# Three more attention groups scored by four strips of 32 rows, with their keys kept in finished output tiles

## The chip, the cores and the metric

The kernel runs on one core of one Trainium2 chip. The metric is the device time of one execution in microseconds. The kernel before takes 632.41 us as the median of 3 runs (631.19 to 633.22).

## The reference

Two independent blocks share the launch; their outputs stand side by side. The first is attention with 16 query heads of width 28 over one shared key and value head. The second is a two-dimensional spectral filter.

```python
B, S, D, H = 1, 2048, 448, 16          # Dh = 28
q = (x @ wq).reshape(B, S, H, Dh).transpose(0, 2, 1, 3)
k = x @ wk;  v = x @ wv                # one head, shared by the 16
scores = einsum("bhqd,bkd->bhqk", q, k) * Dh ** -0.5
o = einsum("bhqk,bkd->bhqd", softmax(scores, -1), v)
a = o.transpose(0, 2, 1, 3).reshape(B, S, H * Dh) @ wo
X = rfft2(x2, axes=(-2, -1)) * (w_r + 1j * w_i)
b = irfft2(X, s=(S, D), axes=(-2, -1))
return concatenate([a, b], -1)
```

## The kernel before, in words

**The stages.** The first 72 us project queries, keys and values and start the forward transform of the spectral block. The rest is one long attention stage, into which the remaining spectral work and the output projections are woven, and a short tail.

**Groups and steps.** The queries are cut into 4 chunks of 512 rows (`c`) and 4 sets of 4 heads (`g`). One pair (c, g) is a group; there are 16, numbered here from the 1st to the 16th in the order of work (the program's own number, `4 * c + g`, starts at 0). A group has 16 steps, one for each block of 128 keys (`kc`), so there are 256 steps. A step makes four score tiles of 128 keys by 512 queries, one for each head, each in one bank of PSUM; exponentiates them on ScalarE into SBUF tiles `p`; and multiplies them with the values `vs` on TensorE into bank 7 (line 1190). Seven banks are left for scores and for other work.

**Two ways to score.** Queries and keys are split into a high and a low part (`qh`, `ql`, `kh`, `kl`), and the score is kh·qh + kh·ql + kl·qh.

- *Strips* (function `strips`, lines 1131 to 1166). Each head has 28 rows in a strip of 32 partitions, and the keys stand four times, once in each strip. The step issues 12 matmuls of 32 rows: three passes over four strips (line 1141). Four strips work side by side in the array. The exponentials of a step are taken of one bank, of two neighbouring banks at once, and of one bank (lines 1155 and 1157), where two of the free banks are neighbours; else of four single banks. The order is strict: one step's strips, then the values of the step two before it.
- *Stacked* (function `score`, line 1119). The three products (and kl·ql) stand below each other in the 128 rows: the keys in one tile `ka` = [kh, kh, kl, kl], the queries of a group in a tile `qa` that holds [qh, ql, qh, ql] of each head. One matmul of 128 rows gives one head's tile, so a step is 4 matmuls, with four exponentials of one bank each (line 1175). `build_q` prepares `qa` of the next group: three VectorE operations (lines 194 to 196) and nine DMAs on SyncE's queue (lines 213 and 214).

Before the change the first 5 groups are strips (`STRIPS = 5`) and the other 11 are stacked. `HOME` names groups whose queries are split straight into a `qa` tile's space.

**What sets the order.** All engines run an order that the program writes out while it is built. A small clock model (`clk`, `free`, `end`) decides in the main loop (from line 1259) when to score, when to multiply with the values and when to put in other TensorE work, which is called a fill here. In stacked groups the values come in blocks of two steps, called a pair here (8 scores, then 2 steps of values), or, where there is work to fill in, in blocks of four steps with up to three or four fills between the scores. The fills are the output projections of finished chunks (`w_unit`, line 1039, 44 matmuls for each of the first three chunks) and the last part of the inverse transform (`z_unit`, `y_unit`, lines 941 and 967). No fill is put into strips. When all scores are issued, the first 36 matmuls of the last chunk's projection follow (`partial`: 12 pieces of 3 matmuls), then the last head set's.

**Where the keys stand.** `kh` and `kl` for strips live in the first buffers of the pools tagged `oh` and `ol`. Each pool has two buffers; the normed outputs of a chunk (`oh[c]`, `ol[c]`) rotate through the same buffers. A chunk's outputs are read for the last time by its output projection.

Of the kernel before, what the change touches and what calls it, by code (L numbers as in the profile page):

```python
# [12 lines left out]
F32 = mybir.dt.float32  # L13
# [19 lines left out]
LEAD = 7  # L33
WARM = 8, 8
FIRST = 8
STRIPS = 5
HOME = {1: 0, 3: 1, 4: 0}
PLACES = (3, 5, 6, 8, 9, 10)


# [57 lines left out]
def kernel(ctx: ExitStack, tc: tile.TileContext, t: dict):  # L98
    nc = tc.nc
# [98 lines left out]
    def build_q(c, g):  # L198
        n = 4 * c + g
        qt = qp.tile([128, CW], F32, name="qt")  # L200
        if n in HOME:
            qh, ql = (slots[HOME[n]][:, p] for p in range(2))
        else:
            qh = qp.tile([128, CW], F32R, name="qh")
            ql = qp.tile([128, CW], F32R, name="ql")
        split_q(qt, qh, ql, c, g)
        if n < STRIPS:
            qa[c, g] = qh, ql
            return
        q = qa[c, g] = slots[n % 2]  # L210
        for i in range(4):
            for p, src in enumerate((qh, ql)):
                nc.sync.dma_start(q[32 * p:32 * p + 32, i].bitcast(F32), src[32 * i:32 * i + 32].bitcast(F32))
        nc.sync.dma_start(q[64:128].bitcast(F32), q[0:64].bitcast(F32))
# [543 lines left out]
    def stacked_keys():  # L758
        for p, k in enumerate((kh, kh, kl, kl)):
            r = slice(32 * p, 32 * p + 32)  # L760
            nc.sync.dma_start(ka[r].bitcast(F32), k[r].bitcast(F32))

    t1v = t1.rearrange("(r k) l u (n f) -> r (k l u) n f", r=2, f=113)

    def spread(i):
# [294 lines left out]
    def w_unit(c, k):  # L1060
        def go(g):
            def f(b):
                wo_mm(bank[b][:, :D], c, k, (g,))
                if g == NG - 1:
                    after(clk["pe"] + 0.9, 0.65, out, b)
            return f

        def out(b):
            wo_out(bank[b][:, :D], c, k)
            free[b] = clk["dve"] + 0.1  # L1070
        return [(0.605 if g else 0.403, go(g)) for g in range(NG)]


# [56 lines left out]

    def strips(st):
        c, g, kc = steps[st]
        bs = heapq.nsmallest(4, range(7), key=free.__getitem__)
        mid = next(((a, a + 1) for a in sorted(bs[:3]) if a + 1 in bs[:3]), None)
        if mid and st:
            bs = [b for b in bs[:3] if b not in mid] + [*mid, bs[3]]
        qh, ql = qa[c, g]
        for n, (k, q) in enumerate(((kh, qh), (kh, ql), (kl, qh))):
            for i in range(4):
                r = slice(32 * i, 32 * i + 32)  # L1140
                mm(bank[bs[i]], k[r, kc * 128:(kc + 1) * 128], q[r], start=(n == 0), stop=(n == 2))  # L1141
        switch("r")
        t0 = clk["pe"] + (0.11 if clk["new"] else 0.0)
        at = []
        for b in bs:
            t0 = max(t0 + 0.005, free[b])
            free[b] = inf
            at.append(t0 + 0.46 + 0.49)
        clk["pe"], clk["new"] = t0 + 0.69, False
        ends, sides = [pp.tile([128, 2, CW], F32, name="p") for _ in range(2)], (0, 3)  # L1150
        for i in range(4):
            pt[4 * st + i] = ends[0][:, i // 3] if i in sides else ends[1][:, i - 1]
        for i, n in ((0, 1), (1, 2), (3, 1)) if mid and st else ((i, 1) for i in range(4)):
            if n == 2:
                nc.scalar.activation(ends[1], banks[:, bs[1]:bs[1] + 2], AF.Exp, scale=SCALE)  # L1155
            else:
                nc.scalar.activation(pt[4 * st + i], bank[bs[i]], AF.Exp, scale=SCALE)  # L1157
            a = max(clk["act"], at[i + n - 1], vend[st - 4] if st > 3 else 0.0)
            clk["act"] = a + (0.904 if n == 2 else 0.49)
            for m in range(i, i + n):  # L1160
                end[4 * st + m] = clk["act"] + 0.163
                free[bs[m]] = clk["act"] + 0.153
        if kc == 0:
            after(clk["pe"] + 3.0, 1.7, build_q, *order[4 * c + g + 1])

    half = []
# [1 line left out]
    def exps():  # L1168

        while waiting and waiting[0][0] < 4 * done_steps + P_BUFS:  # L1170
            i, b, at = waiting.popleft()
            if i % 2 == 0:
                half[:] = [pp.tile([128, 2, CW], F32, name="p")]
            p = pt[i] = half[0][:, i % 2]
            nc.scalar.activation(p, bank[b], AF.Exp, scale=SCALE)  # L1175
            a = max(clk["act"], at, vend[(i - P_BUFS) // 4] if i >= P_BUFS else 0.0)
            clk["act"] = a + 0.490
            end[i] = a + 0.593 + 0.06
            free[b] = a + 0.593 + 0.05

    def values(o, n):
        while taken_out[0] < o // 16:
            vector(clk["dve"] + 0.5)
        switch("v")
        if held[0]:
            piece()
        for st in range(o, o + n):
            c, g, kc = steps[st]
            for i in range(4):
                mm(bank[7][32 * i:32 * i + 32], vs[:, kc], pt.pop(4 * st + i), start=(kc == 0), stop=(kc == 15))  # L1190
            clk["pe"] = max(clk["pe"], end[4 * st + 3]) + 0.86
            vend[st] = clk["pe"] + 0.15
            if kc == 15 and st < 255:
                after(clk["pe"] + 0.4, 0.72, group_out, c, g)
        clk["new"] = False
# [5 lines left out]
    def first_fill():  # L1201
        pb = fft1_mm(FIRST - 1)
        clk["pe"] += 1.0
        free[6] = inf
        fft1_out(FIRST - 1, pb)
        clk["dve"] = max(clk["dve"], clk["pe"] + 0.5) + 1.5
        free[6] = clk["dve"] + 0.1
# [11 lines left out]
        after(1.0 + 3.0 * (q - FIRST), 0.0, late_load, q)  # L1219
        after(6.0 + 9.0 * (q - FIRST), 1.35, late_fold, q, 0)  # L1220

    sc, since, gap = 64 * STRIPS, 0, 2
    parts, tail = deque((k, g) for k in range(4) for g in range(NG - 1)), {}

    def partial():
# [7 lines left out]
        wo_mm(tail[k], NC - 1, k, (g,))  # L1233
        spent(0.605)

    def size():
        left = 16 - done_steps % 16
        rich = sum(map(len, work["w"])) * 0.6 + len(work["z"]) * 0.88 + (len(cur[0][0]) * 0.6 if cur[0] else 0.0) > 1.0
        b = 4 if rich else 2
        return left if left < b + 2 else b  # L1240
# [1 line left out]
    total = 12 * 2.22 + 16 * (0.88 + 0.73)  # L1242

    def share(n):
        return max(1.8, n * (total - done[0]) / max(250 - done_steps, 3)) if n > 2 else 0.0

    done_steps, quota = 0, 0.0
    for k in range(16 * STRIPS):
        if k:
            vector(clk["pe"])  # L1250
        strips(k)
        if k == 0:
            first_fill()
        if k > 1:
            values(done_steps, 1)
            done_steps += 1
            exps()
    n = size()
    while done_steps < 256:
        vector(clk["pe"])  # L1260
        hold()
        need = 4 * (done_steps + n)
        t_v = end[need - 1]
        soon = min(free) <= clk["pe"] + 0.05
        more = sc < 1024
        if t_v <= clk["pe"] + 0.05 and (sc >= min(need + LEAD, 1024) or not soon):
            values(done_steps, n)
            done_steps += n
            exps()
            n = size()  # L1270
            since, gap, quota = 0, 2, share(n)
        elif can_fill() and quota > 0 and since >= EARLY and gap >= 2 and (cur[0] or soon):
            t0 = done[0]
            fill()
            quota -= done[0] - t0
            gap = 0
        elif more and soon:
# [163 lines left out]
```

## Time and profile before

| | us |
|---|---|
| median of 3 runs | 632.41 |
| profiled execution | 635.41 |
| its span | 633.6 |
| TensorE busy | 626.5 |
| ScalarE busy | 543.1 |
| VectorE busy | 343.1 |
| strips, first five groups (start of the second step to the first stacked score) | 75.7 to 227.0 |
| stacked, eleven groups (first stacked score to the last value matmul) | 227.0 to 619.0 |
| tail | 619.0 to 633.6 |

The profiled execution is 3.0 us longer than the median of the runs, and 1.8 us longer than its span. In the timeline a row gives start, duration, engine, line, operation and how many stand in it; the idle time before it stands in brackets with what ended it. One value matmul in the program appears as two in the trace, so "x16" on line 1190 is two steps. Matmuls overlap, so the distance from one start to the next tells the pace, not the sum of the durations.

### The profile page before, as it was taken

How to read it: one execution, taken by the hardware profiler on the slowest of the kernel's cores; microseconds unless marked ns; L12 is line 12 of the kernel's file. 1: busy time of each engine (PE TensorE's matmuls, PEld its weight loads, DVE VectorE, ACT ScalarE, POOL GpSimd, SP SyncE). 2: the span in 40 equal slices, each digit the busy share in tenths (PEclk: the TensorE clock that was granted, in tenths of full speed). 3: DMA queues.
4: the chain of work that ended last, by engine and by line, in shares of the span. 5: the costliest groups of instructions: out<-in, count | busy, mean ns of one | idle time of the engine just before them, and what ended most of it. 6: DMA issues, size and time to landing. Idle time of an engine off the chain costs nothing.

```text
span 633.6 us, 12824 instructions
## 1 busy us (share of the span) xinstructions
PE 626.5 (99%) x4976; PEld 333.5 (53%) x4976; DVE 343.1 (54%) x684; ACT 543.1 (86%) x1023; POOL 90.5 (14%) x167
## 2 busy tenths in 40 slices
PE   8999999999999999999999999999999999999997
PEld 6877633333333346554445656657564446564445
DVE  6898522979788988897732533226462202330104
ACT  4645599999999998789998878888779998889991
POOL 1021130202121201010323012021110101010200
PEclk9999799999999999999999999999999999999999
DMA  8746695001033422130673242152523020140002
GB/s 305 267 127 181 156 251 202 17 19 46 2 94 91 108 52 62 63 82 24 186 247 98 93 116 97 47 145 69 157 82 69 31 68 31 39 108 2 16 1 87
DMA packets 29367, 62.34 MB, mean 98 GB/s; under 512 B 6689, under 2 KB 16257, under 8 KB 28469
## 3 DMA queue, kind: packets, MB, share of 16 engines
q1 hardware_dynamic: 21338, 39.97, 22.1%
q0 software_dynamic: 7536, 20.98, 10.9%
q8 instruction: 39, 0.64, 0.4%
q10 hardware_dynamic: 432, 0.57, 0.2%
q14 instruction: 22, 0.18, 0.1%
HBM read 30.58 MB, written 16.30 MB: 74 GB/s over the span
## 4 chain that ended last, share of the span: by engine, by line
PE 88%; ACT 0%; issue 0%; DVE 0%; ACTq 0%
PE banks L1190 38%; PE banks L1119 28%; PE banks L1141 12%; PE banks L1039 5%; PE banks L941 2%; PE banks L967 2%; PE banks L1318 0%; PE banks L167 0%; ACT p L1155 0%; ACT yb L1054 0%; DVE yb L1057 0%; ACTq L1055 0%; ACT p L1157 0%
## 5 line engine op out<-in xcount | busy, mean ns | idle before, releaser
L1175 ACT ACTIVATE p<-banks 128x512 f32<-128x512 f32 x704 | 350.6, 713 | 38.6 <-PE banks L1190 22.5
L1190 PE MATMUL banks<-p,vs 128*32 128x512 f32 x2048 | 249.6, 599 | 0.0
L1119 PE MATMUL banks<-qa,ka 128*128 128x512 f32 x704 | 196.5, 407 | 0.0
L1119 PEld LDWEIGHTS banks<-qa,ka 128*128 128x128 f32 x704 | 124.7, 188 | 79.9 <-ACT p L1175 56.4
L1190 PEld LDWEIGHTS banks<-p,vs 128*32 128x32 f32 x2048 | 51.8, 109 | 116.4 <-issue 113.6
L1157 ACT ACTIVATE p<-banks 128x512 f32<-128x512 f32 x168 | 93.4, 624 | 2.7 <-PE banks L1141 2.6
L1155 ACT ACTIVATE p<-banks 128x1024 f32<-128x1024 f32 x76 | 79.4, 1045 | 0.0
L996 DVE COPY qraw<-banks 128x512 f32<-128x512 f32 x15 | 10.4, 692 | 72.4 <-PE banks L1190 72.4
L1001 POOL DMA_DIRECT2D sd<-qraw x15 | 9.0, 597 | 256.7 <-DVE qraw L996 256.7
L1043 DVE COPY ya<-banks 128x448 f32<-128x448 f32 x12 | 7.5, 625 | 67.3 <-PE banks L1039 34.0
L1141 PEld LDWEIGHTS banks<-qa,kh 32*128 32x128 f32 x384 | 14.5, 183 | 40.2 <-ACT p L1157 40.2
L1141 PE MATMUL banks<-qa,kh 32*128 32x512 f32 x384 | 35.5, 441 | 0.0
L824 DVE SCALAR_TENSOR_TENSOR X<-w,X 128x226 f32<-128x226 f32 (+2 forms) x72 | 34.1, 473 | 2.4
L1009 POOL DMA_DIRECT2D R<-rd x60 | 30.5, 515 | 30.5 <-DMA rd<-rs 30.5
L973 DVE COPY w<-banks 128x256 f32<-128x256 f32 x16 | 6.8, 424 | 37.4 <-PE banks L967 36.7
L327 ACT ACTIVATE qraw<-banks 128x512 f32<-128x512 f32 x16 | 9.4, 599 | 19.2 <-PE banks L323 19.1
L323 PE MATMUL banks<-xh,wqh 128*128 128x512 f32 x64 | 24.6, 417 | 0.6 <-DVE xh L271 0.6
L323 PE MATMUL banks<-xh,wql 128*128 128x512 f32 x64 | 23.2, 394 | 0.0
L949 DVE CAST zh<-banks 113x512 fp32r<-113x512 f32 (+1 forms) x16 | 11.0, 688 | 21.3 <-ACT p L1175 17.6
L1039 PE MATMUL banks<-woh,oh 128*128 128x448 f32 x60 | 22.2, 370 | 0.0
L1039 PE MATMUL banks<-wol,oh 128*128 128x448 f32 x60 | 21.9, 365 | 0.0
L1141 PEld LDWEIGHTS banks<-qh,kh 32*128 32x128 f32 x128 | 7.0, 190 | 27.9 <-ACT p L1157 25.1
(130 smaller groups left out, 701.2 us busy)
## 6 DMA issues: line engine op xcount, KB each, us to landing
qa<-qa SPq DMA_DIRECT2D x11, 512.0 KB
xb<-xb SPq DMA_DIRECT2D x8, 512.0 KB
ob<-yo SPq DMA_DIRECT2D x16, 256.0 KB
t<-bs SPq DMA_DIRECT2D x16, 226.0 KB
X<-t POOLq DMA_DIRECT2D x8, 452.0 KB, 12.7
wf<-w POOLq DMA_DIRECT2D x8, 452.0 KB, 3.7
c<-t POOLq DMA_DIRECT2D x8, 452.0 KB, 4.0
R<-rd POOLq DMA_DIRECT2D x60, 56.0 KB, 2.2
```

Source lines behind the costliest of these rows:

```text
L323: mm(pq[c, g], w[:, j, gs], x[:, j], start=(j == 0 and n == 0), stop=(j == 3 and n == 1))
L824: todo(226 * n, lambda d=d, q=q: STT(both(d), t[0].rearrange("p r n f -> p r (n f)"), q, both(a), op0=ALU.mult, op1=ALU.add))
L941: mm(pz[:w, j], fb["c2", q % 2][:, e, j, :w], fb["fi", q % 2][:, j], start=True, stop=True)
L967: mm(py[:, k], c[:w, kind], z, start=(n == 0), stop=(n == 2))
L1009: nc.gpsimd.dma_start(R[32 * i:32 * i + DH], rd[i:i + 1].to_broadcast([DH, CW]))
L1039: mm(p, x[c][:, g, s], w[:, m], start=(g == 0 and n == 0), stop=(g == NG - 1 and n == 2))
L1119: mm(bank[b], ka[:, kc * 128:(kc + 1) * 128], qa[c, g][:, h], start=True, stop=True)
L1141: mm(bank[bs[i]], k[r, kc * 128:(kc + 1) * 128], q[r], start=(n == 0), stop=(n == 2))
L1155: nc.scalar.activation(ends[1], banks[:, bs[1]:bs[1] + 2], AF.Exp, scale=SCALE)
L1157: nc.scalar.activation(pt[4 * st + i], bank[bs[i]], AF.Exp, scale=SCALE)
L1175: nc.scalar.activation(p, bank[b], AF.Exp, scale=SCALE)
L1190: mm(bank[7][32 * i:32 * i + 32], vs[:, kc], pt.pop(4 * st + i), start=(kc == 0), stop=(kc == 15))
```

## The change

The set of strip groups becomes a list: the first five groups and the 8th, 13th and 16th (program numbers 7, 12, 15). `kh` and `kl` no longer exist when these run, so their keys are copied: as soon as a chunk's output projection has read its `oh` and `ol` tiles for the last time, four DMAs on SyncE's queue (`copy_keys`) fill these two tiles with kh and kl, four strips each, from the stacked `ka`. The first chunk's tiles serve the 8th group, the second's the 13th, the third's the 16th. The queries of the three groups go straight into a `qa` tile's space on VectorE, without the nine DMAs each.

The main loop now enters strips when all earlier scores are issued and the values are at most two steps behind; it issues them without fills, and it sizes blocks of stacked steps so that they end at the entrance. The weight that spreads the fills over the steps (`share`) now counts up to step 234, not 250.

```diff
-STRIPS = 5
-HOME = {1: 0, 3: 1, 4: 0}
+STRIPS = 0, 1, 2, 3, 4, 7, 12, 15
+HOME = {1: 0, 3: 1, 4: 0, 7: 1, 12: 0, 15: 1}
+KEYS = {7: 0, 12: 1, 15: 2}
...
-        if n < STRIPS:
+        if n in STRIPS:
             qa[c, g] = qh, ql
             return
...
+    spread_keys = {-1: (kh, kl)}
+
+    def copy_keys(c):
+        spread_keys[c] = [x[c].rearrange("p g n -> p (g n)") for x in (oh, ol)]
+        for k, d in enumerate(spread_keys[c]):
+            for u in range(2):
+                nc.sync.dma_start(d[64 * u:64 * u + 64].bitcast(F32), ka[64 * k:64 * k + 64].bitcast(F32))
...
             wo_out(bank[b][:, :D], c, k)
             free[b] = clk["dve"] + 0.1
+            if k == 3:
+                after(clk["dve"] + 0.5, 0.0, copy_keys, c)
...
         c, g, kc = steps[st]
+        kh, kl = spread_keys[KEYS.get(4 * c + g, -1)]
...
-        if kc == 0:
+        if kc == 0 and st < 240:
             after(clk["pe"] + 3.0, 1.7, build_q, *order[4 * c + g + 1])
...
+    def limit():
+        return min([16 * g for g in STRIPS if 64 * g >= sc] + [256])
+
     def size():
         left = 16 - done_steps % 16
+        if done_steps < limit() - 2:
+            left = min(left, limit() - 2 - done_steps)
...
-        return max(1.8, n * (total - done[0]) / max(250 - done_steps, 3)) if n > 2 else 0.0
+        return max(1.8, n * (total - done[0]) / max(234 - done_steps, 3)) if n > 2 else 0.0
...
-    for k in range(16 * STRIPS):
-        if k:
-            vector(clk["pe"])
-        strips(k)
-        if k == 0:
-            first_fill()
-        if k > 1:
-            values(done_steps, 1)
-            done_steps += 1
-            exps()
-    n = size()
+    sc = 0
     while done_steps < 256:
+        k = sc // 4
+        if 4 * k == sc and k // 16 in STRIPS and k < 256 and (done_steps >= k - 2 or not k):
...
+            if k:
+                vector(clk["pe"])
+            strips(k)
+            sc += 4
+            if k == 0:
+                first_fill()
+            while done_steps <= k - 2:
+                values(done_steps, 1)
+                done_steps += 1
+                exps()
+            n, since, gap, quota = size(), 0, 2, 0.0
+            continue
...
-        more = sc < 1024
-        if t_v <= clk["pe"] + 0.05 and (sc >= min(need + LEAD, 1024) or not soon):
+        more = sc < 4 * limit()
+        if t_v <= clk["pe"] + 0.05 and (sc >= min(need + LEAD, 4 * limit()) or not soon):
```

What this does to the order is shown at three places. The first is TensorE at the entrance into the 8th group. `qa_1071` and `qa_1072` are the two query tiles, `p,vs` are values (x8 is two steps, x4 one). Before:

```order
L1190 MATMUL banks<-p,vs 32x512 x8
L1119 MATMUL banks<-qa_1071,ka 128x512 x8
L1190 MATMUL banks<-p,vs 32x512 x8
L1119 MATMUL banks<-qa_1071,ka 128x512
L1119 MATMUL banks<-qa_1072,ka 128x512 x7
L1190 MATMUL banks<-p,vs 32x512 x8
L1119 MATMUL banks<-qa_1072,ka 128x512 x8
```

There one pair follows the other across the border of the groups. The same place now:

```order
L1202 MATMUL banks<-p,vs 32x512 x8
L1130 MATMUL banks<-qa_1071,ka 128x512 x8
L1202 MATMUL banks<-p,vs 32x512 x8
L1130 MATMUL banks<-qa_1071,ka 128x512
L1153 MATMUL banks<-qa_1072,oh 128x512 x8
L1153 MATMUL banks<-qa_1072,ol 128x512 x4
L1202 MATMUL banks<-p,vs 32x512 x4
L1153 MATMUL banks<-qa_1072,oh 128x512 x8
```

After the last score of the 7th group come 12 strip matmuls for each step, with the keys in `oh` and `ol`, and one step of values between. At the exit the order is the one that the kernel before has once, after its 5th group: 7 scores, then 2 steps of values.

The second place is SyncE's queue at the end of the first chunk's projection (`ya` are its output rows). Before:

```order
L1025 DMA lows<-ol 128x512
L1045 DMA oa<-ya 128x448
L213 DMA qa_1072<-qh 32x512
L213 DMA qa_1072<-ql 32x512
...
L214 DMA qa_1072<-qa_1072 64x2048
L1045 DMA oa<-ya 128x448
L213 DMA qa_1071<-qh 32x512
```

Now:

```order
L1034 DMA lows<-ol 128x512
L1054 DMA oa<-ya 128x448 x2
L770 DMA oh<-ka 64x2048 x2
L770 DMA ol<-ka 64x2048 x2
L214 DMA qa_1071<-qh 32x512
```

The nine DMAs that built the 8th group's queries are gone, and four copies of 64 rows with 2048 elements each stand behind the last output row block.

The third place is the end of TensorE's order. Before:

```order
L1119 MATMUL banks<-qa_1072,ka 128x512 x8
L1190 MATMUL banks<-p,vs 32x512 x8
L1119 MATMUL banks<-qa_1072,ka 128x512
L1039 MATMUL banks<-woh,oh 128x448
L1039 MATMUL banks<-wol,oh 128x448
L1039 MATMUL banks<-woh,ol 128x448
L1190 MATMUL banks<-p,vs 32x512 x8
L1039 MATMUL banks<-woh,oh 128x448
```

Now:

```order
L1153 MATMUL banks<-qa_1072,oh 128x512 x8
L1153 MATMUL banks<-qa_1072,ol 128x512 x4
L1202 MATMUL banks<-p,vs 32x512 x4
L1048 MATMUL banks<-woh,oh 128x448
L1048 MATMUL banks<-wol,oh 128x448
L1048 MATMUL banks<-woh,ol 128x448
L1048 MATMUL banks<-woh,oh 128x448
L1048 MATMUL banks<-wol,oh 128x448
L1048 MATMUL banks<-woh,ol 128x448
L1202 MATMUL banks<-p,vs 32x512 x8
```

Before, the three matmuls ahead of the last values are the last piece of the third chunk's projection, and all 12 pieces of the fourth chunk's follow behind the values. Now that piece has gone into the 15th group, two pieces of the fourth chunk's stand ahead of the last values and ten behind them.

Over the whole attention stage, the stacked blocks of four steps with fills stay 23; the pairs go from 43 to 19 (the last one without scores); and 48 steps are strips. ScalarE's exponentials of one bank go from 872 to 782 and those of two banks from 76 to 121.

More of the change, by code (lines that the diff above doesn't have):

```diff
@@ L1220 @@
         after(6.0 + 9.0 * (q - FIRST), 1.35, late_fold, q, 0)
-    sc, since, gap = 64 * STRIPS, 0, 2
+    sc, since, gap = 0, 0, 2
     parts, tail = deque((k, g) for k in range(4) for g in range(NG - 1)), {}
@@ L1244, in share @@
     def share(n):
-        return max(1.8, n * (total - done[0]) / max(250 - done_steps, 3)) if n > 2 else 0.0
+        return max(1.8, n * (total - done[0]) / max(234 - done_steps, 3)) if n > 2 else 0.0
     done_steps, quota = 0, 0.0
-    for k in range(16 * STRIPS):
-        if k:
-            vector(clk["pe"])
-        strips(k)
-        if k == 0:
-            first_fill()
-        if k > 1:
-            values(done_steps, 1)
-            done_steps += 1
-            exps()
-    n = size()
-    while done_steps < 256:
+    sc = 0
+    while done_steps < 256:
+        k = sc // 4
+        if 4 * k == sc and k // 16 in STRIPS and k < 256 and (done_steps >= k - 2 or not k):
+            assert not waiting and KEYS.get(k // 16, -1) in spread_keys
+            if k:
[10 more added lines that the diff above has]
+            continue
         vector(clk["pe"])
```

## The prediction

> **What bounds the kernel now.** I read the page first, then the stretches of the span, then the timeline of ScalarE in a strip step, then the chain of waits.
>
> ```profile
> span 633.6 us, 12824 instructions
> ...
> PE 626.5 (99%) x4976; PEld 333.5 (53%) x4976; DVE 343.1 (54%) x684; ACT 543.1 (86%) x1023; POOL 90.5 (14%) x167
> ```
>
> TensorE (PE) works 99% of the span and ScalarE (ACT) 86%: two engines near their limit, so a share of busy time does not say which one a change must relieve. The stretches do (span, then busy time and instructions of PE, weight loads, DVE, ACT, POOL, granted clock, DMA share, GB/s):
>
> ```profile
> 281.00:336.00 55.00, 55.00 (x341) 25.79 (x337) 33.39 (x100) 55.00 (x115) 10.89 (x19) 1.00 0.44 140
> ...
> 350.00:477.00 127.00, 127.00 (x852) 78.94 (x848) 58.58 (x113) 105.09 (x210) 17.61 (x31) 1.00 0.34 100
> ```
>
> From 281 to 336 us stacked groups run in pairs without fills, and both engines are full: 55.00 of 55 us each. From 350 to 477 us there are fills; ScalarE falls to 105.09 of 127 us and TensorE alone is the bound. In strips ScalarE sets the pace:
>
> ```profile
> 101.35 1.07 ACT L1155 ACTIVATE p<-banks 128x1024 f32<-128x1024 f32 x1
> 102.25 1.15 ACT L1157 ACTIVATE p<-banks 128x512 f32<-128x512 f32 x2
> 103.24 1.08 ACT L1155 ACTIVATE p<-banks 128x1024 f32<-128x1024 f32 x1
> ```
>
> From start to start the two-bank exponential takes 0.90 us and the two single ones 0.99 us (0.495 each) with no idle time between: 1.89 us for a step. The chain of waits (start, duration, what) gives the paces over many steps:
>
> ```profile
> 79.89 1.00 PE banks L1190 x8
> ...
> 129.25 0.99 PE banks L1190 x8
> ...
> 244.45 3.57 PE banks L1190 x32
> 248.02 1.58 PE banks L1119 x6
> 254.17 3.57 PE banks L1190 x32
> ...
> 281.32 2.04 PE banks L1119 x8
> ...
> 332.12 2.07 PE banks L1119 x8
> ...
> 572.51 2.10 PE banks L1119 x8
> ...
> 612.15 2.11 PE banks L1119 x8
> 614.26 1.85 PE banks L1190 x16
> 617.16 1.85 PE banks L1190 x16
> 619.02 7.53 PE banks L1039 x36
> 626.55 2.27 PE banks L1318 x6
> ```
>
> - Strips: 26 steps from 79.89 to 129.25, so 1.898 us a step, the pace of ScalarE above.
> - Pairs in the middle: 13 from 281.32 to 332.12, so 3.908 us a pair, 1.954 a step.
> - Pairs in the 15th and 16th group: 10 from 572.51 to 612.15, so 3.964 us a pair. Why these are 0.056 slower I do not know; ScalarE does eight exponentials in it, 0.4955 each, its strip figure, so I take them to be bound by ScalarE.
> - Four-step blocks with fills: 9.72 us (244.45 to 254.17).
>
> **The change, part by part.**
>
> *Steps.* By the written order the 23 blocks with fills stay 23. Of the 42 pairs with scores 18 are left: 13 pairs of the fast kind and all 11 of the slow kind go, 13 x 3.908 + 11 x 3.964 = 94.4 us. In their place come 48 strip steps, 48 x 1.898 = 91.1 us. That is -3.3 us. A strip step's 12 matmuls, three passes over four strips, replace four of 128 rows on TensorE; this saves TensorE time, but ScalarE allows only the difference between two and one exponential call for two banks, 2 x 0.495 - 0.90 = 0.09 us a step. The order has 45 two-bank calls more for the 48 steps, so three steps miss this: +0.3 us in all, which I take in. If the three pairs left near step 234 run at the slow pace, +0.2 us; I leave that for the range.
>
> *Fills.* The three matmuls of the third chunk's last piece, which now stand ahead of the last values, move into a block with fills: 3 x 7.53 / 36 = 0.21 us each, +0.6 us there. The other fills only change places among 23 blocks, in which they are on TensorE's path before and after.
>
> *Entrances and exits.* The one exit that the trace has, at the end of the 5th group, costs ScalarE nothing:
>
> ```profile
> 227.55 0.60 ACT L1157 ACTIVATE p<-banks 128x512 f32<-128x512 f32 x1
> 228.03 4.54 ACT L1175 ACTIVATE p<-banks 128x512 f32<-128x512 f32 x9
> ```
>
> There is no bracket, so no idle time: the two new exits I cost at 0. No entrance is in the trace. There the strips write four banks in three passes, so the first exponential must wait for the third pass, while ScalarE has only the scores that lie in the other banks. The nearest row is ScalarE's wait for first scores after a long block of values:
>
> ```profile
> 346.62 9.42 ACT L1175 ACTIVATE p<-banks 128x512 f32<-128x512 f32 x19 [0.39 <-PE banks L1119]
> ```
>
> So 0 at the one end, and at the other this wait and a whole step of values as well, 0.39 + 1.00 (first row of the chain). A gain is excluded, since ScalarE does the same calls. I take 0.2 us, between none and 0.39, since a pair leaves some scores waiting: 3 x 0.2 = +0.6 us; ends 0 and +4.2 us.
>
> The Trainium skill, TensorEngine Tiling (Array Packing), Key Properties, says that a change of the tiling mode drains TensorE. A drain's price can be read here: a block of four steps of values takes 3.57 us, two blocks of two steps 2 x 1.85, so a block costs 0.13 us beside its work. A strip step changes mode twice, a pair twice in two steps; by the rule as a charge on top, 48 more changes x 0.13 = +6.2 us. By the row the sum stays, since the 1.898 us of a strip step were measured with its changes inside, behind ScalarE. The row decides.
>
> *The keys.* Four copies for each of the three groups, 512 KB each, from `ka` to the freed tiles, 64 rows of 8 KB. The kernel issues a copy of this very shape for each stacked group (line 214):
>
> ```profile
> 236.42 0.51 SPq L214 DMA_DIRECT2D qa<-qa  x1
> ...
> 273.97 0.57 SPq L1045 DMA_DIRECT2D oa<-ya  x1
> ```
>
> ```profile
> 237.00:238.00 1.00, 1.00 (x16) 0.26 (x8) 1.00 (x2) 1.00 (x3) 0.00 (x0) 1.00 0.60 131
> 238.00:239.00 1.00, 1.00 (x10) 0.48 (x3) 0.97 (x2) 1.00 (x3) 0.00 (x0) 1.00 1.18 246
> 239.00:240.00 1.00, 1.00 (x6) 0.78 (x5) 1.00 (x2) 1.00 (x4) 0.00 (x0) 1.00 0.69 147
> ```
>
> Issued at 236.42, it moves 131 + 246 + 147 = 524 KB in these three microseconds, at full load some 246 KB a microsecond. Four in a row: 0.6 us until the first moves and 4 x 524 / 246 = 8.5 us, or 4 x 3 = 12 us if they don't overlap; 9 to 13 us.
> For the 8th group the copies stand behind the output row block issued at 273.97; by the written order the entrance comes at least five pairs, 19.5 us, later, and 9 to 13 us are needed. For the 13th some 26 steps, over 49 us, lie between. The tight one is the 16th: from the projection's last matmul to the entrance lie four scores, four steps of values (3.57) and three pairs (11.7), some 16 us; needed are an estimated 2 us for the last row block's eviction and issue, and 9 to 13. I cost the copies at 0: the cover is these 16 us, and if it is gone the strips wait, and with them ScalarE, which has no other scores left. SyncE's queue loses 27 DMAs and gains 12; behind the copies stand only output rows and query loads for a later group.
> The Trainium skill, DMA: Bandwidth & Descriptors (Where 436 GB/s comes from), has SBUF to SBUF bound by the fabric at about 435 GB/s; by it four copies would take an estimated 4.8 us. The row, 246, does not reach that, and I plan with the row; the page only makes a late key less likely.
>
> *The end.* Before, from the start of the values at 614.26 plus 1.85, that is 616.11, to 626.55 pass 10.44 us. Now follow two pieces of the fourth chunk (7.53 / 12 = 0.63 each), the last values 1.85, ten pieces 6.3 and about 0.2 for changes: 9.6 us, so -0.8 us. It falls to 0 if the last values wait for the last exponentials, and I keep that for the range. Next late would be VectorE, which norms the last head set for the four matmuls behind the pieces:
>
> ```profile
> 626.04 0.29 DVE L1316 TENSOR_TENSOR qraw<-qraw,r 128x128 f32<-128x128 f32 x1
> ```
>
> It is done 7.3 us after the start of the pieces at 619.02. Now the pieces take 6.3 us and three of the four last matmuls (2.27 us for three) come before the one that needs it: 8.6 us, so it stays off the path.
>
> *Sum.* -3.3 + 0.3 + 0.6 + 0.6 - 0.8 = -2.6 us. The profiled execution would go from 635.41 to 632.8; it lies 3.0 us above the median of the runs. Against that median: 632.41 - 2.6 = 629.8 us, 0.4% faster. A measurement of this kernel can tell about 0.3%, 1.9 us, from no change.
>
> **The rivals.**
>
> - *The seams eat it.* Each entrance costs ScalarE the upper end, 1.39 us in place of 0.2, +3.6 us: 633.4 us, and at half of that 631.6, within 0.3%. For it: seven banks, of which a step takes four at once, and both engines full. Against it: the exit shows no gap, and strips run at ScalarE's pace with the same seven banks.
> - *Late keys, slower.* The 16th group's strips wait at the entrance for their copies. Up to 16 us after the last projection matmul nothing happens; each further microsecond is one of span. To be 1.9 us slower than before they must come 4.5 us late: 2.6 us to the first byte and 18 us of moving, 116 KB a microsecond, half of the row's rate. At 100 KB: 21 us of moving, 7.4 late, 629.8 + 7.4 = 637.2 us. For it: four copies in one queue. Against: no other large transfer is near.
> - *The seams cost nothing* and the end saves all: -3.3 + 0.3 + 0.6 - 0.8 = -3.2 us, 629.2; with the three singles hidden too, -3.5, 628.9.
> - *The drains come on top* (+6.2 us, 636.0): nothing in the strips of the first five groups speaks for it, 26 steps at 1.898.
>
> **How the numbers follow.** My forecast, a seam near 0.2 us, 0.45; cheap seams 0.20; dear seams 0.24; late keys 0.08; drains 0.03. The first two end below -1.9 us but for the spread of the runs (631.19 to 633.22), which takes some 0.05 off to "same"; of the dear seams 0.04 end above +0.3%, 0.06 below -0.3%. Faster 0.66, same 0.19, slower 0.15. The range goes from 627.8 (cheap seams, 1 us of spread) to 632.6 (dear seams in part, the slow pairs and an end that saves nothing).
>
> **What would show it.** Right: 1.90 us a step in the chain in the 8th, 13th and 16th group; no wait for a DMA at their first strip matmul; ScalarE without idle time from one end of these groups to the other; TensorE's pieces behind the last values 30, not 36. Wrong: idle time of ScalarE over 0.5 us at an entrance (seams); a wait of the strips for the copies (keys); strip steps near 2 us (drains, or exponentials that find no neighbours); or longer blocks with fills, if these wait for data that the order now asks for earlier.

## The result, and the profile after

The changed kernel takes 629.96 us as the median of 18 runs (628.12 to 633.87), the kernel before in the same comparison 632.34 us (18 runs, 630.71 to 636.38). The ratio is 0.9958, 95% interval [0.9943, 0.9973]. Compared once more, later, it was 0.9976 [0.9962, 0.9990]. So the gain is some 0.2 to 0.4%; the forecast was 0.4%, 629.8 us.

The two profiled executions differ by 633.6 - 627.9 = 5.7 us in span, and not all of this is the change's. In the timeline the first stacked score starts at 226.99 us before and at 223.71 after: 3.3 us lie ahead of the first thing that was changed. They are not the change's: in e6_share and e7_finish below, which are the kernel before up to there, this score starts at 223.70 and 223.54 (the last section says what a part of the 3.3 us is). From the first stacked score to the end of the span it takes 406.61 us before and 404.19 after, **2.42 us less**. This stretch, called the stage from here on, is what the runs below are compared by; it was 404.15 in the second profile of the changed kernel. Its end is not sharp: behind the start of VectorE's last copy the span still holds the last store, 3.41 us before and 3.39 after, but from 3.07 to 3.43 over the runs below. Up to that copy it takes 403.20 us before, 400.80 and 400.81 in the two profiles after.

First the page of the kernel after, then its chain of waits (start, duration, what; line 1130 is the stacked score, 1153 strips, 1202 values, 1048 the projection):

```profile
span 627.9 us, 13612 instructions
...
PE 621.0 (99%) x5360; PEld 318.8 (51%) x5360; DVE 343.0 (55%) x684; ACT 540.1 (86%) x978; POOL 90.2 (14%) x167
```

```profile
294.97 0.99 PE banks L1202 x8
...
319.66 0.99 PE banks L1202 x8
...
572.66 2.04 PE banks L1130 x8
...
576.55 2.07 PE banks L1130 x8
...
583.69 1.00 PE banks L1202 x8
...
602.70 1.00 PE banks L1202 x8
...
611.29 1.42 PE banks L1048 x6
612.71 1.85 PE banks L1202 x16
614.56 6.30 PE banks L1048 x30
620.87 2.27 PE banks L1340 x6
```

TensorE is as full as it was, 99%. In the 8th group 13 steps go by between 294.97 and 319.66, 1.899 us each; in the 16th 10 steps between 583.69 and 602.70, 1.901 each. The pair from 572.66 to 576.55 takes 3.89 us, where pairs at this place took 3.964 before. At the end, 9.58 us pass from the first piece of the projection (611.29) to line 1340 (620.87); before, it was 10.44 from the end of the values (616.11), with the last stacked score and one piece more in it.

### The profile page after: what moved, and what is told of

Its sections match the earlier page's. It is cut to its first block, busy times and chain, and to the rows that moved or that the text cites. A ratio compares the mean times of both kernels' runs of the same rounds, so it can differ in the third digit from the quotient of the medians.

```text
span 627.9 us, 13612 instructions
## 1 busy us (share of the span) xinstructions
PE 621.0 (99%) x5360; PEld 318.8 (51%) x5360; DVE 343.0 (55%) x684; ACT 540.1 (86%) x978; POOL 90.2 (14%) x167
## 4 chain that ended last, share of the span: by engine, by line
PE 88%; ACT 0%; issue 0%; DVE 0%; ACTq 0%
PE banks L1202 39%; PE banks L1130 20%; PE banks L1153 19%; PE banks L1048 6%; PE banks L950 2%; PE banks L976 2%; PE banks L1340 0%; PE banks L168 0%; ACT p L1167 0%; ACT yb L1063 0%; DVE yb L1066 0%; ACTq L1064 0%; ACT p L1169 0%
## 5 line engine op out<-in xcount | busy, mean ns | idle before, releaser
L1187 ACT ACTIVATE p<-banks 128x512 f32<-128x512 f32 x512 | 256.4, 692 | 40.0 <-PE banks L1202 18.9
L1202 PE MATMUL banks<-p,vs 128*32 128x512 f32 x2048 | 254.5, 600 | 0.0
L1169 ACT ACTIVATE p<-banks 128x512 f32<-128x512 f32 x270 | 151.8, 637 | 2.2 <-PE banks L1153 2.1
L1130 PE MATMUL banks<-qa,ka 128*128 128x512 f32 x512 | 145.8, 407 | 0.0
L1167 ACT ACTIVATE p<-banks 128x1024 f32<-128x1024 f32 x121 | 128.2, 1060 | 0.0
L1130 PEld LDWEIGHTS banks<-qa,ka 128*128 128x128 f32 x512 | 90.6, 188 | 52.7 <-ACT p L1187 34.1
L1202 PEld LDWEIGHTS banks<-p,vs 128*32 128x32 f32 x2048 | 49.3, 108 | 112.8 <-issue 109.5
L1153 PE MATMUL banks<-qa,oh 32*128 32x512 f32 x384 | 35.5, 441 | 0.0
L1153 PEld LDWEIGHTS banks<-qa,oh 32*128 32x128 f32 x384 | 14.5, 183 | 38.5 <-ACT p L1169 37.7
```

Source lines behind the costliest of these rows:

```text
L1130: mm(bank[b], ka[:, kc * 128:(kc + 1) * 128], qa[c, g][:, h], start=True, stop=True)
```

## Experiments

Eleven runs. Each ratio is to the kernel before as it was timed in the same comparison (medians 632.34, 631.91, 631.08 and 631.24 us). The stage is read from each run's profile, once to the end of the span and once to the start of VectorE's last copy; a difference of some tenths of a microsecond there is seen in no median.

| run | what it is | median us (runs) | ratio to before | stage us | to last copy us |
|---|---|---|---|---|---|
| before | | 632.34 (18) | | 406.61 | 403.20 |
| after | the change | 629.96 (18) | 0.9958 [0.9943, 0.9973] | 404.19 | 400.80 |
| e10_after_again | the change | 629.19 (12) | 0.9976 [0.9962, 0.9990] | 404.15 | 400.81 |
| e6_share | before, fills' weight alone | 630.91 (11) | 0.9978 [0.9959, 0.9998] | 405.50 | 402.07 |
| e7_finish | before, one piece earlier | 630.96 (12) | 0.9990 [0.9973, 1.0007] | 405.96 | 402.54 |
| e3_mid | 8th and 13th group alone | 630.66 (12) | 0.9975 [0.9956, 0.9993] | 405.64 | 402.57 |
| e2_last | 16th group alone | 629.35 (8) | 0.9958 [0.9937, 0.9978] | 404.61 | 401.40 |
| e1_single | four single exponentials | 630.05 (12) | 0.9977 [0.9960, 0.9993] | 405.82 | 402.49 |
| e5_two_pass | two passes, not three | 627.06 (7) | 0.9932 [0.9910, 0.9954] | 403.21 | 399.87 |
| e4_twice | each key copy twice | 646.45 (4) | 1.0222 [1.0180, 1.0265] | 421.63 | 418.53 |
| v_8 | 9th group too | 629.12 (13) | 0.9964 [0.9948, 0.9980] | 404.70 | 401.30 |
| e8_nine_pairs | v_8, more two-bank calls | 627.91 (6) | 0.9953 [0.9935, 0.9971] | 403.91 | 400.48 |
| e9_more_pairs | after, more two-bank calls | 629.53 (12) | 0.9974 [0.9959, 0.9988] | 404.09 | 400.73 |

**Which engine sets a strip step?** The prediction said ScalarE. Two runs ask it from both sides. The first gives ScalarE more to do: the 48 added steps take four single exponentials.

```diff
-        mid = next(((a, a + 1) for a in sorted(bs[:3]) if a + 1 in bs[:3]), None)
+        mid = next(((a, a + 1) for a in sorted(bs[:3]) if a + 1 in bs[:3]), None) if st < 80 else None
```

> The changed kernel with four exponentials of one bank each in the three added groups, nothing else. Theory, ScalarE sets the pace of a strip step: it goes from 1.898 to four times 0.495, 1.98 us, +3.8 us on the 45 steps: 633.8, slower than the kernel before by 1.4 us. Rival, the saved TensorE work carries the gain: 630.0 as the changed kernel.

The second gives TensorE less to do in these steps, and leaves out kl·qh.

```diff
-        for n, (k, q) in enumerate(((kh, qh), (kh, ql), (kl, qh))):
+        passes = ((kh, qh), (kh, ql), (kl, qh))[:3 if st < 80 else 2]
+        for n, (k, q) in enumerate(passes):
```

> The changed kernel with two of the three strip passes in the three added groups: the product kl x qh is left out there, so the scores of these groups are less exact. The run with single exponentials has changed the theory: there the first strip steps still took 1.90 us with four single calls, so TensorE, not ScalarE, sets the 1.90 us. Theory now: ScalarE stands close behind at 0.90 + 2 x 0.49 = 1.88 us, so a step falls by 0.02 us only, -1 us in 48 steps: 629. Rival, ScalarE has more room: TensorE's step falls by a pass of 0.23 us to 1.67 us, -11 us: 619.

The timeline of TensorE in the run with four singles: the first two steps of the 8th group, and two later ones that are two steps apart.

```profile
292.19 0.74 PE L1153 MATMUL banks<-qa,oh 32*128 32x512 f32 x8
...
294.09 0.73 PE L1153 MATMUL banks<-qa,oh 32*128 32x512 f32 x8
...
305.58 0.82 PE L1153 MATMUL banks<-qa,oh 32*128 32x512 f32 x8
...
309.50 0.81 PE L1153 MATMUL banks<-qa,oh 32*128 32x512 f32 x8
```

The same in the run with two passes:

```profile
292.08 0.74 PE L1154 MATMUL banks<-qa,oh 32*128 32x512 f32 x8
...
293.75 0.74 PE L1154 MATMUL banks<-qa,oh 32*128 32x512 f32 x8
...
304.79 0.97 PE L1154 MATMUL banks<-qa,oh 32*128 32x512 f32 x8
...
312.37 0.97 PE L1154 MATMUL banks<-qa,oh 32*128 32x512 f32 x8
```

With four singles a step still takes 294.09 - 292.19 = 1.90 us at first, as long as ScalarE may fall behind; then it takes 1.96 (two steps from 305.58 to 309.50). So 1.90 us is what TensorE needs, and ScalarE with four singles is the slower of the two. With two passes the first step takes 1.67 us, which is TensorE's pace with one pass less (0.23 us); then four steps take 304.79 to 312.37, 1.895 each, and it is ScalarE that sets this pace. So a strip step with a two-bank call has two limits, TensorE's 1.90 and ScalarE's 1.895, that happen to coincide. That ScalarE alone sets it is wrong. In the stage four singles cost 405.82 - 404.19 = 1.6 us, where 3.8 were expected; two passes save 1.0, as expected.

The profile tells the two cases apart, and it did so before the change. ScalarE's exponentials in groups (the number after the bar is the busy time, then the mean ns of one): the kernel before in its first strips (101 to 215 us), in the pairs of the middle (281 to 335), and in its last pairs (575 to 612); then the run with two passes in the 8th group (304 to 318).

```profile
L1157 ACT ACTIVATE p<-banks 128x512 f32<-128x512 f32 x122 | 68.3, 625 | 0.0
```

```profile
L1175 ACT ACTIVATE p<-banks 128x512 f32<-128x512 f32 x113 | 55.5, 953 | 0.0
```

```profile
L1175 ACT ACTIVATE p<-banks 128x512 f32<-128x512 f32 x76 | 37.8, 626 | 0.0
```

```profile
L1170 ACT ACTIVATE p<-banks 128x512 f32<-128x512 f32 x16 | 12.2, 1041 | 0.0
```

It is the same instruction on the same shape, and from start to start it takes 0.48 to 0.50 us in all of them; yet its recorded duration is 625 ns or 1041 ns. What is above some 0.6 us I read as waiting inside the engine; no run takes the two apart. Where work piles up before ScalarE (two passes, 1041; pairs of the middle, 953) durations are long; where it is fed just in time (strips, 625; last pairs, 626) they are short. "Idle 0.0" and "busy 100%" stand beside all of them and tell nothing. The height alone is not the pace, though: in the last pairs of e6_share and e7_finish below, which run at the same 3.90 to 3.91 us, the medians are 963 and 681 ns. What they share is growth, from 800 to 1022 ns and from 624 to 731 between the first windows (574 to 582 us) and the last (606 to 612), where the slow pairs before stay at 616 to 628.

**How much of the gain are the strips?** The diff also changed a number in the weight of the fills. One run makes this edit alone in the kernel before:

```diff
-        return max(1.8, n * (total - done[0]) / max(250 - done_steps, 3)) if n > 2 else 0.0
+        return max(1.8, n * (total - done[0]) / max(234 - done_steps, 3)) if n > 2 else 0.0
```

> The kernel before with one edit: the weight of the fills counts up to step 234 in place of 250; no group more is strips. Theory: part of the gain is not the strips'. In the kernel before the third chunk's last output projection stays unfinished from about step 232 to the end and holds one of the seven score banks, so the last pairs run at 3.964 us on six banks; with the weight changed it is finished before, the last eleven pairs run at 3.908 us (-0.6 us), and two pieces of the fourth chunk's projection move ahead of the last values (-0.8 us at the end, +0.6 us in the blocks with fills): -0.8 us, 631.5 against a median of 632.3. Rival, the whole gain belongs to the strips: the pairs stay at 3.964 us and the time within 0.3 us of the kernel before.

The stage falls by 406.61 - 405.50 = 1.11 us without a single new strip. Its chain of waits at the end:

```profile
573.25 2.04 PE banks L1119 x8
...
608.38 2.07 PE banks L1119 x8
...
612.73 1.22 PE banks L1039 x6
613.96 1.85 PE banks L1190 x16
615.81 6.32 PE banks L1039 x30
622.13 2.27 PE banks L1318 x6
```

Nine pairs from 573.25 to 608.38 take 3.903 us each, no longer 3.964, and six matmuls of the last chunk's projection stand ahead of the last values, as in the changed kernel. So the slow pairs were not made slow by ScalarE's own pace. In the written order before, one piece of the third chunk's projection is left over, and its bank is held, half summed, from step 232 until the last values (the program's `fill` sets `free[b] = inf` until the sum is complete and copied out); scores then go round on six banks, not seven. With the other weight the piece is done in time.

The next run tests this story by moving only this piece: in the kernel before, it goes between the scores of the first pair after step 232.

```diff
-        elif can_fill() and quota > 0 and since >= EARLY and gap >= 2 and (cur[0] or soon):
+        elif can_fill() and (quota > 0 or 232 <= done_steps < 236) and since >= EARLY and gap >= 2 and (cur[0] or soon):
```

> The kernel before with one piece (three matmuls) of the third chunk's output projection moved from the end into the first pair after step 232, and nothing else; two pieces of the fourth chunk's then stand ahead of the last values. Theory: the unfinished projection held one of seven score banks; freed, the last ten pairs run at 3.91 in place of 3.964 us, -0.6 us, and the end gains 0.2 us: -0.8 us, 631.2. Rival, the slow pairs have another cause (the place in the program, the short span of VectorE's work): they stay at 3.964 us, and the time within 0.3 us of the kernel before.

The pairs after it take 3.89 to 3.92 us and the stage 405.96, 0.65 us less than before. Ten pairs at 0.06 and the end (10.44 us to 9.82) would be -1.2; the +0.6 left over stands for the piece itself. So the trace shows that the unfinished piece makes these pairs slow; that it does so through its bank is read from the program. In the time nothing is shown, since 0.9990 [0.9973, 1.0007] holds no change.

**Which groups?** Two runs leave out groups: one has only the 8th and 13th, with the old weight of 250; one has only the 16th, with the new weight.

```diff
-STRIPS = 0, 1, 2, 3, 4, 7, 12, 15
+STRIPS = 0, 1, 2, 3, 4, 7, 12
```

> The changed kernel with only the 8th and the 13th group added (the weight at 250 as before). Theory: 16 pairs of 3.908 us against 32 strip steps of 1.898 us, -1.8 us, two entrances +0.4 us, no gain at the end: -1.4 us, 630.9. The pairs of the last two groups stay at 3.964 us, the unfinished projection holds its bank. Rival, the seams eat it: within 0.3 us of the kernel before.

```diff
-STRIPS = 0, 1, 2, 3, 4, 7, 12, 15
+STRIPS = 0, 1, 2, 3, 4, 15
```

> The changed kernel with only the 16th group added to the strips (the weight at 234). Theory: what the weight alone gives (-0.8 us) and 8 pairs of 3.908 us in exchange for 16 strip steps of 1.898 us (-0.9 us), an entrance +0.2 us: -1.5 us, 630.8. Rival, the 16th group carries the whole gain by its slow pairs and the end: -2.4 us.

To the end of the span the 8th and 13th group alone save 0.97 us and the 16th with the weight 2.00. Here the last store matters: it takes 3.07 us in e3_mid and 3.21 in e2_last. Up to VectorE's last copy the parts are -0.63 for the 8th and 13th group (the pairs of the last two groups stay at 3.96 to 3.97 there), -1.13 for the weight alone, and -1.80 for the 16th with the weight, so -0.67 for the group. Together they are -2.43, and the changed kernel has -2.40: the parts add up.

The 16th group gives the 0.7 us that were expected of it, the 8th and 13th only 0.63 of 1.4. The rest is lost in the 23 blocks with fills. Adding up the stacked score matmuls in these blocks (each row of scores from its first start to the start of what follows it), 367 take 91.75 us before and 364 take 91.71 in e3_mid; three fewer should save 3 x 0.25. The pair with the new weight says the same: 366 take 91.02 in e6_share, 363 take 91.00 in the changed kernel, while e2_last, without the 8th and 13th group, has 366 in 91.03. Why these scores take 0.7 us longer, no run shows.

**The copies of the keys.** Here every copy is issued twice:

```diff
-            for u in range(2):
+            for u in (0, 1, 0, 1):
```

> The changed kernel with each key copy issued twice, so 8 copies of 512 KB per group in place of 4. Theory: the copies' cover is used up to 3.7 us: in the changed kernel's trace those for the 16th group are issued from 565.2 and move until 577.1, and its strips start at 580.8. Twice as many move until some 588.5, 7.7 us late; those for the 8th group, issued at 270.5 and done near 284, until 297, 3 us after its strips' start at 294.0. Together +10.7 us: 641. Rival, the copies could move at 435 GB/s and have room: no change, 630.

The timeline of TensorE at the entrance into the 16th group and at 449 us, and of SyncE's queue:

```profile
589.12 0.74 PE L1153 MATMUL banks<-qa,oh 32*128 32x512 f32 x8
592.76 0.79 PE L1153 MATMUL banks<-qa,ol 32*128 32x512 f32 x2 [2.91 <-DMA ol<-ka]
596.09 0.79 PE L1153 MATMUL banks<-qa,ol 32*128 32x512 f32 x2 [2.54 <-DMA ol<-ka]
```

```profile
448.91 2.54 PE L1130 MATMUL banks<-qa,ka 128*128 128x512 f32 x5 [5.36 <-DVE zl L959]
```

```profile
419.08 18.19 SPq L770 DMA_DIRECT2D ol<-ka  x4
437.32 19.30 SPq L994 DMA_DIRECT2D ob<-yo  x6
```

At the 16th group the strips wait for `ol`, as expected, and the last stacked score and the first step take 10.00 us instead of 2.34. At the 8th group the keys, expected 3 us late, are in time. What was not expected is the wait at 449 us, where no strips are near. The doubled copies of the second chunk occupy SyncE's queue until 437; behind them stand six stores of the spectral block's output. Until the first of them have gone, VectorE waits for an output buffer (9.6 us in two waits), does not empty a bank, and TensorE stands still for 5.4 us. So the price of a long DMA is also what stands behind it in its queue; the prediction had counted the output rows there as harmless. The stage is 17.4 us longer than the changed kernel's, where 10.7 were expected. By the times at which the same steps of values start, some 1.5 us are lost in the 8th group, 7.0 around 449 us and 9.2 at the 16th group. The last two hold a loss that neither the keys nor the queue shows: the clock granted to TensorE fell to 0.50 from 449 to 451 us and from 592 to 601, and the second step of the 16th group takes 3.44 us.

**A version with more of it.** The 9th group is made strips as well, with the first chunk's tiles:

```diff
-STRIPS = 0, 1, 2, 3, 4, 7, 12, 15
+STRIPS = 0, 1, 2, 3, 4, 7, 8, 12, 15
```

> The changed kernel with the 9th group as strips as well, from the same keys as the 8th; the fills move into fewer blocks. Theory: 8 pairs of 3.908 us more go for 16 strip steps of 1.898 us, -0.9 us against the changed kernel, no further entrance: 629.1. Rival: the fills are denser, three or four in a block with five or more pieces, and some wait for transfers of the inverse transform or for a bank: no gain or a loss up to 2 us.

It brought nothing: stage 404.70, half a microsecond longer than with the change. The 13th group found no two neighbouring banks free in any of its steps and took four singles. So the choice of banks was widened, to the four earliest in place of three, first with the 9th group and then without it:

```diff
-        if mid and st:
+        if st >= 80 and not mid:
+            mid = next(((a, a + 1) for a in sorted(bs) if a + 1 in bs), None)
+            if mid:
+                bs = [b for b in bs if b not in mid][:1] + [*mid] + [b for b in bs if b not in mid][1:]
+        if mid and st and set(mid) <= set(bs[:3]):
```

> The changed kernel with the 9th group as strips too (as in v_8) and a choice of banks that takes two neighbouring free banks wherever the four free ones hold them, so that 139 exponentials of two banks stand in the order in place of 123, and every strip step of the 8th, 9th, 13th and 16th group has one. Theory: a strip step is 1.90 us where a two-bank call stands in it and 1.96 us where all four are single; so the 13th group, which ran at 1.96 in v_8, goes back to 1.90: 16 x 0.06 = -1.0 us against v_8, and the 9th group's 16 steps save 8 pairs x (3.91 - 3.80) = -0.9 us against the changed kernel, less 0.2 for the pairs that are lost beside fills: some 629 us or a little below, ratio near 0.995. Rival: the gain of more strips is given back in the blocks with fills, which are the same in number over fewer pairs: first stacked score to end 404.7 us as in v_8 or more, no gain over the changed kernel.

> The changed kernel with the same choice of banks alone: 124 exponentials of two banks in place of 121, the three strip steps without one get theirs. Theory: 3 x 0.06 = -0.2 us, not to be told from the changed kernel; it is the run that e8_nine_pairs is compared with. Rival: the other banks free later and the steps wait: slower than the changed kernel by over 0.5 us from first stacked score to end (404.2 us).

> The changed kernel again, unaltered, on the chip of these runs: 404.2 us from the first stacked score to the end of the span, and a ratio near 0.996 to the kernel before.

ScalarE's timeline in the 13th group, first with the old choice of banks, then with the new:

```profile
477.68 9.00 ACT L1169 ACTIVATE p<-banks 128x512 f32<-128x512 f32 x18
```

```profile
478.84 1.02 ACT L1171 ACTIVATE p<-banks 128x1024 f32<-128x1024 f32 x1
...
484.54 1.02 ACT L1171 ACTIVATE p<-banks 128x1024 f32<-128x1024 f32 x1
```

Eighteen singles stood in a row; now three steps go by from 478.84 to 484.54, 1.90 us each. The stage falls from 404.70 to 403.91, 0.8 of the 1.0 us expected. Against the changed kernel (404.15 in the same comparison) it is 0.2 us, 0.3 up to the last copy, where some 0.7 were expected. The median of 627.91 us is the lowest of any run that computes everything, but its interval overlaps that of the changed kernel in the same comparison (0.9953 [0.9935, 0.9971] and 0.9976 [0.9962, 0.9990]), and the trace accounts for 0.2 or 0.3 of the 1.3 us between them. That it beats the changed kernel is not shown. The wider choice alone gives 404.09, nothing that can be told.

## Why the prediction was right

The time, 629.96 for 629.8, came out of terms of which some held, one held for another reason, and some were off in ways that cancelled; two readings behind them were wrong.

- *Steps, -3.3 us.* The size held: strip steps at 1.899 and 1.901 us where 1.898 was put. **The step that failed is "In strips ScalarE sets the pace".** TensorE needs 1.90 us for a strip step by itself, as the runs with four singles and with two passes show. I drew from the small saving that "ScalarE allows only" 0.09 us a step; a faster ScalarE would have allowed nothing more, and what the strips save is TensorE's time. The error did no harm, because the pace was measured on strips with both engines in it.
- *Slow pairs.* "I take them to be bound by ScalarE" is wrong; the ground for it was 8 x 0.4955 us, starts that ScalarE makes when it is fed just in time. The rows said so: 626 ns mean duration there against 953 in the middle. The cause is the unfinished piece and, by the program, its held bank. With 11 x 0.056 = 0.6 us this part of the -3.3 is due to the weight of the fills and not to strips.
- *Three steps without a two-bank call, +0.3 us.* By the run with four singles a step without the call costs 0.06 us more once ScalarE is behind, and nothing in a group's first steps; the wider choice of banks gave back 0.1 us or less. The term was too large, by little.
- *The piece among the fills, +0.6 us.* It holds in the run that moves this piece alone. With the new weight alone, -0.6 for the pairs and -0.6 at the end leave only about +0.1 for it. The two can't be separated further in the changed kernel.
- *The other fills, 0.* That they "only change places" was put at nothing and cost 0.7 us: the scores in the 23 blocks take as long as before though there are fewer of them, wherever the 8th and 13th group are strips.
- *Entrances, +0.6 us.* TensorE's and ScalarE's timeline at the entrance into the 8th group of the kernel after:

```profile
293.56 0.50 PE L1130 MATMUL banks<-qa,ka 128*128 128x512 f32 x1
294.00 0.74 PE L1153 MATMUL banks<-qa,oh 32*128 32x512 f32 x8
...
295.90 0.73 PE L1153 MATMUL banks<-qa,oh 32*128 32x512 f32 x8
```

```profile
289.16 5.86 ACT L1187 ACTIVATE p<-banks 128x512 f32<-128x512 f32 x11
295.06 0.60 ACT L1169 ACTIVATE p<-banks 128x512 f32<-128x512 f32 x1
295.55 1.02 ACT L1167 ACTIVATE p<-banks 128x1024 f32<-128x1024 f32 x1
```

From 293.56 to 295.90 TensorE does one stacked score and one strip step in 2.34 us; that is 0.44 more than a strip step, and a score is worth 1.82 / 7 = 0.26 by the row of seven at 223.78 to 225.60 in the chain. So the change of the way to score costs about 0.2 us, on TensorE; ScalarE shows no bracket, and the rival of the dear seams fell. So did the rival of the drains: the new groups run at 1.90 us a step, with the changes of mode inside.

- *Exits, 0.* At 324.4 us TensorE does 7 scores and 2 steps of values in 3.67 us, as it does at 227 us in the kernel before.
- *The keys, 0.* SyncE's queue after the third chunk's projection, the windows of a microsecond (the last number is GB/s), and the strips of the 16th group:

```profile
565.21 1.13 SPq L770 DMA_DIRECT2D oh<-ka  x2
566.43 4.40 SPq L770 DMA_DIRECT2D ol<-ka  x2
```

```profile
574.00:575.00 1.00, 1.00 (x8) 0.39 (x10) 0.00 (x0) 1.00 (x3) 0.00 (x0) 1.00 1.13 246
...
577.00:578.00 1.00, 1.00 (x6) 0.77 (x6) 0.00 (x0) 1.00 (x3) 0.00 (x0) 1.00 0.10 38
578.00:579.00 1.00, 1.00 (x7) 0.34 (x9) 0.00 (x0) 1.00 (x3) 0.00 (x0) 1.00 0.00 0
```

```profile
580.84 0.74 PE L1153 MATMUL banks<-qa,oh 32*128 32x512 f32 x8
```

Issued from 565.21 on, the copies move until some 577.1: 12 us, the upper part of the 9 to 13 that were estimated; the strips start 3.7 us later and wait for nothing. The cover is real and not large: 3.7 us of some 16. The Trainium skill, DMA: Bandwidth & Descriptors (Where 436 GB/s comes from), puts the limit for a transfer within SBUF at about 435 GB/s; no microsecond of these copies reaches more than 246.

- *The end, -0.8 us.* From the end of the values before to the last four matmuls, 10.44 us became 9.58: -0.86. In the run with the weight alone a part of it, 0.6, is already there: that is the piece, which now stands among the fills. The other 0.25 is the last stacked score.
- *Sum.* -1.54 us up to the end of the values before, where -1.8 were put, and -0.88 from there: -2.42 for -2.6. The order of the fills has about 1.1 of it. That the total came so close is partly luck: the piece among the fills and the three single steps were put some 0.7 us too dear, the blocks with fills 0.7 us too cheap.

## What to carry to other kernels

A busy engine without idle time need not be the limit: follow one instruction's recorded duration along a stage, for where it grows with the same shape and the same pace of starts, work piles up before the engine, and where it stays short, the engine is being fed just in time. When a diff changes both the work and a number that spreads other work, run the number alone; here it had almost half of the gain. Add up the parts to a point that the last store does not blur. And price a long DMA not by its bytes alone, but by what stands behind it in its queue.

## What the runs showed of the hardware

The two profiles of the changed kernel differ by 1.6 us, 627.9 and 626.3, with stages of 404.19 and 404.15. Windows of one microsecond around 70 us (the third number from the end is the granted clock), first after, then after again, then before:

```profile
70.00:71.00 1.00, 1.00 (x12) 0.54 (x6) 1.00 (x2) 0.31 (x1) 0.00 (x0) 0.50 0.10 16
...
73.00:74.00 1.00, 1.00 (x14) 0.77 (x14) 0.99 (x2) 0.08 (x1) 0.84 (x2) 0.83 0.86 180
```

```profile
70.00:71.00 1.00, 1.00 (x20) 0.60 (x17) 1.00 (x2) 0.71 (x2) 0.00 (x0) 1.00 0.00 0
```

```profile
70.00:71.00 1.00, 0.93 (x16) 0.83 (x20) 0.00 (x0) 0.49 (x1) 0.00 (x0) 0.90 0.91 181
...
77.00:78.00 1.00, 0.76 (x6) 0.04 (x2) 0.93 (x3) 0.63 (x2) 0.00 (x0) 0.69 0.91 154
```

In one execution of the same program the clock is halved for some 3.4 us (0.50 in the windows from 70 to 73, 0.96 and 0.83 beside them), in another not at all; in the kernel before it is halved for some 6.8 us, twice as long (0.50 in the windows from 71 to 77). Between the two executions of the changed kernel the first strips start at 69.62 and 69.59, and the first stacked score at 223.71 and 222.15: 1.6 us, about what 3.4 us at half the clock lose. So of the 5.7 us between the first two profiles, over half was not the change's, and part of that was the clock; a forecast against one profiled execution has to begin where the change begins. The Trainium skill, TensorE: Matmul & The Clock Gate (Part 1: The HAM clock gate), has the clock halve after an idle window of about 3.4 us. The length agrees with these rows. That TensorE was idle for so long ahead of it does not: the longest wait that the timeline shows there is 0.44 us. In the run with doubled copies the clock did fall where TensorE stood still: at the end of the wait of 5.36 us it is 0.75 in the window from 448 and 0.50 in the next, and in the wait that ends at 592.76 it is 0.93 in the window from 591 and 0.50 in the next, some 2 us after TensorE's last work at 589.86. So the rows show the halving with a long wait and without one.
